# An attention and SwiGLU kernel: one ScalarE instruction without its wait for VectorE, three sums placed elsewhere in the last visits, one output scaled by another engine, and one step more in halves

## The chip, the cores and the metric

The kernel runs on one core of a Trainium2 chip. A core has five engines that work side by side, each through its own instructions in order: TensorE (PE; its weight loads are shown as PEld), VectorE (DVE), ScalarE (ACT), GpSimd (POOL) and SyncE (SP, which here only issues transfers). They wait for each other by semaphores. Matrix products are written to PSUM, which has eight banks of 512 fp32 values in each of 128 partitions; all else lies in SBUF. The metric is the device time of one execution in microseconds, the median of several runs.

## The reference

Attention without a mask over 8 batches and 12 heads, 448 positions of 64 values, then a SwiGLU feed-forward block over the 3584 tokens:

```python
def _attn_ref(q, k, v):                       # (8, 12, 448, 64) each
    scale = 1.0 / np.sqrt(q.shape[-1])
    scores = scale * np.matmul(q, k.transpose(0, 1, 3, 2))
    scores = scores - np.max(scores, axis=-1, keepdims=True)
    attn = np.exp(scores)
    attn = attn / (np.sum(attn, axis=-1, keepdims=True) + 1e-09)
    return np.matmul(attn, v).astype(np.float32)
...
def _moe_ref(x, w_gate, w_val, w_out):        # (3584, 768), (768, 1536) twice, (1536, 768)
    g = x @ w_gate
    silu = g * (1.0 / (1.0 + np.exp(-g)))
    val = x @ w_val
    return (silu * val @ w_out).astype(np.float32)
...
    x = np.ascontiguousarray(attn_out.transpose(0, 2, 1, 3)).reshape(B * S, H * D)
    return _moe_ref(x=x, **moe_kwargs)
```

## The kernel before

Heads are taken in 48 pairs, six pairs to a batch. Two batches make one block of 896 tokens for the feed-forward part; there are four such blocks. While TensorE works on the attention of later batches, it does the feed-forward of earlier ones in between, so that it always has something to do.

**Attention.** A pair's scores come in chunks (tile `s`, a PSUM tile of two banks from the pool `ps_s`, which has three buffers). ScalarE turns each chunk into exponentials (tile `E`, line 378, and line 403 for the first pairs). Then TensorE multiplies them with the values (tile `acc`, line 462; one bank of the pool `ps_f`, which has two buffers, for each head of the pair), VectorE forms the reciprocal of the row sums (line 504) and normalises (line 505, tile `xt`), and a transposing transfer from SyncE (lines 550 and 556) puts the result into `X`. Values are copied to their place by VectorE (`vo`, line 221).

**The plan.** A loop over `plan` visits three score chunks at a time and at most one pair's accumulation. From the visit called `base` on, what each visit does beside the attention is written out by hand in the list `VISITS`, 33 entries `(begins, nf, ng, no, ns)`: `nf` feed-forward steps, `ng` groups (`OutPair.wide`), `no` pieces of output (`plain_out`), `ns` sums taken from a queue (`add_sum`). The seven visits before `base` have their own list, `FIRST_STEPS`. All instructions are emitted in this order; nothing reorders them afterwards.

**A feed-forward step** (`Step`) forms 128 rows of the gate and value products for 384 or 512 tokens: six matmuls into `gp` (`X` times a gate weight), six into `vp`, both on line 610. ScalarE takes tanh of half of `gp` into `sg` (line 637 for a whole step), VectorE forms `t1 = (sg + 1) * gp` (line 687; the profile calls the tile `t`), then `hts = t1 * vp` (line 693). There are three forms. `run_fv` does one whole step, `run_pair` two interleaved, and `halves()` one step in two halves of the tokens: gate half 0 into one bank of a `ps_s` tile, gate half 1 into the other, then the value halves into two `ps_f` buffers. Its tanh is line 670, its t1 line 672, one of each for each half. A visit that has one step and an accumulation to do (`lone`) uses `halves()`; 17 steps do. `halves()` keeps a list `readers` of the instructions that have read the gate tile, and the helper `apart` takes away the dependencies of the next gate half's matmuls on them. The second tanh is not in that, so it waits for the first half's t1. `late_exp` holds exponentials back: in some visits of 384-token steps the third chunk's exponential is emitted only after the tanhs.

**Output.** `plain_out` multiplies `hts` with the output weights (tile `op`, line 729) and scales the result into `osb`, by VectorE (line 737) where the flag `by_vector` is set, otherwise by ScalarE (line 739). Other token chunks go in pairs through `OutPair.wide`, which forms four 128-row products with seven instead of eight half-size ones (tiles `og`, from `ps_s`, and `ob`, from `ps_f`, line 756). It needs sums of `hts` (four for each pair of chunks, lines 593 to 596) and of the output weights, and it has combines on VectorE (lines 813 and 822) between its products, for which later products wait.

**The last two blocks** are done after the visits by `Unit` (tile `un` from `ps_s`, `ub` from `ps_f`, line 912), in the same manner with seven products instead of eight. For that it needs sums of tokens, `token_sums` (lines 1095 to 1098, four sums of 1344 elements, in the queue `tsums6`), and sums of weights (lines 875 to 878, by GpSimd). The first combine of the first unit is line 961. The four token sums for the third block are popped from `tsums6` one by one in the last visits, at the end of each visit.

Of the kernel before, what the change touches and what calls it, by code (L numbers as in the profile page):

```python
# [12 lines left out]
AF = mybir.ActivationFunctionType  # L13
# [52 lines left out]
def kernel(  # L66
# [10 lines left out]
    nc = tc.nc  # L77
# [521 lines left out]
    class Step:  # L599
# [60 lines left out]
        def halves(self):  # L660
            w = self.at[2] // 2
            parts = [ds(i * w, w) for i in range(2)]
            gs = ps_s.tile([128, 2, 512], FP32, tag="s", name="gp")
            self.sg = fp.tile([128, 512], FP32, tag="sg", name="sg")
            self.t1 = fp.tile([128, 512], FP32, tag="t1", name="t1")
            readers = []
            for i, part in enumerate(parts):
                g = gs[:, i, 0:w]
                apart(self.group("g", gs[:, i], range(NCB), (i * w, w)), *readers)
                readers.append(nc.scalar.activation(self.sg[:, part], g, AF.Tanh, scale=0.5))  # L670
                readers.append(
                    nc.vector.scalar_tensor_tensor(self.t1[:, part], self.sg[:, part], 1.0, g, ALU.add, ALU.mult)
                )
            while late_exp:
                late_exp.pop(0)()
            vps = [ps_f.tile([128, 512], FP32, tag="f", name="vp") for _ in parts]
            for i, vp in enumerate(vps):
                self.group("v", vp, range(NCB), (i * w, w))
            for i, vp in enumerate(vps):
                self.close(i * w, w, vp)  # L680
# [38 lines left out]
    by_vector = [False]  # L719
# [281 lines left out]
    with tc.manual_schedule():  # L1001
# [41 lines left out]
        fvq = []  # L1043
# [8 lines left out]
        def add_block(i, visits):  # L1052
# [36 lines left out]
        ]  # L1089

        def token_sums(x, w, t, eng=nc.vector):
# [131 lines left out]
        g = FIRST * NC  # L1223
# [38 lines left out]
        for x, (chunks, todo) in enumerate(plan):  # L1262
            if not chunks and x > 1:
                break
            quads = [u for u in chunks if u[0] >= QUAD and u[1] == RU]
            split = 0 <= base - x < 3
            rests = [p0 for _, p0 in todo if p0 >= QUAD and not split]
            ordered = quads + [u for u in chunks if u not in quads]
            if (QUAD + 2, RU) in quads:
                ordered = ordered[1:] + quads  # L1270
            small = bool(quads)
            begins, nf, ng = VISITS[x - base][:3] if x >= base else (0, 0, 0)
            if begins > 2:
                add_block(begins, 0)
            lone = nf == 1 and bool(todo) and not split
            behind = []
            for n, (pr, c) in enumerate(ordered if x else []):
                if ng and not todo:
                    behind.append((pr, c, small))
                    continue  # L1280
                if n == 2 and ordered[n] in quads:
                    rests = open_products(rests, small)
                late = n == 2 and not todo and c < NC and pr < QUAD and bool(fvq) and not fvq[0].at[1]
                late = late or n == 2 and lone and not fvq[0].at[1]
                qk(pr, c, small, late)
            if (NPAIR - 1, KR - 1) in chunks:
                load_table("silu_and_others")
            open_products(rests, small)
            if x == 2:
                for t in qk16s:  # L1290
                    nc.vector.memset(t[96:128, 1], 0.0)
                turn_rests(0)
            end = min([y for y in adds if y > x] + [len(plan) + 1])
            if x == 0:
                add_block(0, end)
            early = [p0 for p0 in vcopies.get(x, []) if p0 < QUAD or x > base]
            for p0 in early if x <= base else []:
                copy_v(p0)
            entered = [pr for pr, c in chunks if c == 0]
            ready = []  # L1300
            for pr in entered:
                lead = [pr + 3] if pr + 3 < QUAD else [pr + 3, pr + 4] if pr + 3 == QUAD else [pr + 4]
                for p in lead:
                    if NPE <= p < NPAIR and p not in QPE:
                        ready.append(prep(p))
                if 14 <= pr + LA < NPAIR:
                    load_qk16(pr + LA, 1)
                if 12 <= pr + 3 < NPAIR:
                    load_v(pr + 3)
            for pr, c in chunks:  # L1310
                if c == 2 and (pr < NPE - 2 or pr + 2 in QPE):
                    prep(pr + 2)()
            if x in adds and 0 < x < base:
                add_block(adds[x], end - x)
            for _, p0 in todo:
                if split:
                    pv_split(p0)
                else:
                    pv(p0)
                if p0 < XPE:  # L1320
                    turns.append(p0)
                elif fvq and fvq[0].at[0] < p0 // NHP // NB - 1:
                    held.append(p0)
                else:
                    turn_x(p0)
            for turn in ready:
                if turn:
                    turn()
            for p0 in vcopies.get(x, []):
                if p0 not in early:  # L1330
                    copy_v(p0)
            for pr in entered:
                for w in wq.pop(pr, []):
                    emit(w)
            bare = not todo and bool(chunks) and x > 0
            if 0 < base - x <= len(FIRST_STEPS):
                n = FIRST_STEPS[x - base]
                gate_small[0] = bare
                if n > 1:
                    run_pair()  # L1340
                else:
                    run_fv(True)
            elif x < base:
                if bare and oq and not fvq:
                    carry -= run_o()
                elif bare:
                    gate_small[0] = True
                out_small[0] = not fvq and bool(oq) and any(p0 >= QUAD for _, p0 in todo)
                extra = 2 * fvq[0].time if bare and len(chunks) == 3 and fvq and not fvq[0].at[1] else 0
                carry = run_budget(left() / (end - x) + carry + extra) - extra  # L1350
            else:
                begins, nf, ng, no, ns = VISITS[x - base]
                gate_small[0] = bare
                out_small[0] = bool(no) and not bare
                for _ in range(ng):
                    run_group(behind)
                if lone:
                    fvq.pop(0).halves()
                    add_sum()
                elif bare_next(x):  # L1360
                    for _ in range(nf):
                        run_fv()
                else:
                    run_steps(nf)
                by_vector[0] = True
                for _ in range(no):
                    run_o()
                    out_small[0] = True
                out_small[0] = False
                if begins == 2:  # L1370
                    add_block(2, 0)
                ahead = {3: (x + 1, x + 2), 2: (), 1: ()}.get(len(VISITS) + base - x, (x + 1,))
                for p0 in [p for y in ahead for p in vcopies.get(y, [])]:
                    copy_v(p0)
                add_sum(ns)
                if x == len(VISITS) + base - 6:
                    wsum_space(rfree[:, 2 * NK * S :], 3)
                    for t in qk16s:
                        wsum_space(t[:].rearrange("p t c h d -> p (t c h d)"), 2)
                    wsum_space(Eall, 4)  # L1380
                    tsums6.extend(token_sums(X[KL - 1], S, t6))
            if len(VISITS) + base - x in (5, 3, 2, 1):
                tsums6.pop(0)()
            for u in {len(VISITS) + base - 6: range(2), len(VISITS) + base - 2: range(2, 3)}.get(x, []):
                weight_sums(u)
            while held and not fvq:
                turn_x(held.pop(0))
            while turns:
                turn_x(turns.pop(0))
# [138 lines left out]
```

## Time and profile before

| | |
|---|---|
| Time, median of 3 runs | 427.55 us (427.33 to 427.94) |
| The profiled execution: time | 428.34 us |
| The profiled execution: span of its instructions | 426.6 us |
| Busy in the span: TensorE, VectorE, ScalarE, GpSimd | 416.5, 268.7, 247.9, 224.8 us |
| First visit of `FIRST_STEPS` to the last step, some 84 to 243 us | 159 us, TensorE busy for 157.75 |
| Last visits, 243 to 277 us | 34 us, TensorE busy for 31.94 |
| The two unit blocks, 277 to 426 us | 149 us, TensorE busy for 145.24 |

Times in the profile are counted from the span's start. An engine is named with the line of the kernel and the tiles that an instruction writes and reads, and equal instructions that follow each other closely are merged into one row (x8). In square brackets stands how long the engine stood idle before the row, and what ended that. A matmul's end is modelled, so TensorE can look busy through a short wait; then the row is longer than another one of the same kind.

### The profile page before, as it was taken

Reading aid. Unit: us, or ns where it says so; the run is one execution under the profiler, and the core shown is the slowest. Engines: PE = TensorE matmul, PEld = TensorE weight load, DVE = VectorE, ACT = ScalarE, POOL = GpSimd, SP = SyncE. Lnnn points to the kernel's source line nnn. Section 1 sums busy time; section 2 is a strip of 40 time slices with the busy share of each in tenths; the row PEclk is TensorE's granted clock in tenths of the full one; section 3 lists DMA queues with packets and bytes.
Section 4 is the critical chain, followed back from the end, with each engine's and each line's share of the span. In section 5 each row is a group of like instructions: output and inputs, shape, how many; then the busy total and the mean of one; then the engine's idle time right before and its main releaser. Section 6 shows DMA issues by size and latency. Waiting matters only on the chain.

```text
span 426.6 us, 10831 instructions
## 1 busy us (share of the span) xinstructions
PE 416.5 (98%) x4328; PEld 258.8 (61%) x4328; DVE 268.7 (63%) x613; ACT 247.9 (58%) x384; POOL 224.8 (53%) x343
## 2 busy tenths in 40 slices
PE   8999999999999999999999999899999999999995
PEld 3666666555557776777767676455555655555564
DVE  4667662785777674567745587765765575565562
ACT  6975667646776574777647686545553225545221
POOL 8656625997899965599876625499800000000000
PEclk9999999999999999999999999999999999999999
DMA  9999999999999999999999836610000341000125
GB/s 138 180 201 200 200 176 184 140 162 184 174 189 159 157 208 170 118 167 159 125 166 171 98 76 95 155 35 0 2 1 20 93 116 33 0 2 0 38 79 145
DMA packets 108468, 50.30 MB, mean 118 GB/s; under 512 B 60416, under 2 KB 105344, under 8 KB 108416
## 3 DMA queue, kind: packets, MB, share of 16 engines
q0 software_dynamic: 46800, 24.56, 49.4%
q1 hardware_dynamic: 61344, 24.79, 31.9%
q8 instruction: 34, 0.56, 0.6%
q10 hardware_dynamic: 272, 0.25, 0.2%
q14 instruction: 18, 0.15, 0.1%
HBM read 49.55 MB, written 11.01 MB: 142 GB/s over the span
## 4 chain that ended last, share of the span: by engine, by line
PE 89%; DVE 4%; DMA 2%; POOL 2%; ACT 1%; issue 1%; ACTq 0%; DVEq 0%; POOLq 0%
PE gp L610 14%; PE un L912 13%; PE vp L610 11%; PE ub L912 10%; PE og L756 9%; PE acc L462 8%; PE ob L756 7%; PE s L356 5%; PE op L729 4%; PE acc L426 2%; PE op L1106 2%; PE s L393 2%; DMA qkraw<-in_k_dram 2%; PE s L368 1%; POOL qkraw L203 1%
## 5 line engine op out<-in xcount | busy, mean ns | idle before, releaser
L378 ACT ACTIVATE E<-s 128x896 f16<-128x896 f32 x126 | 106.7, 920 | 32.8 <-PE s L356 25.2
L610 PE MATMUL gp<-X,wg 128*128 128x256 f16 (+3 forms) x390 | 61.7, 304 | 0.0
L610 PE MATMUL vp<-X,wv 128*128 128x256 f16 (+3 forms) x390 | 58.6, 293 | 0.0
L240 POOL COPY qk<-qkraw 128x512 f16<-128x512 f16 x70 | 44.2, 678 | 24.9 <-DMA qkT<-qk 23.2
L180 POOL DMA_DIRECT2D vraw<-in_v_dram x72 | 44.1, 636 | 15.5 <-DMA wo<-in_moe_w_out_dram 8.2
L610 PEld LDWEIGHTS <-wv 128*128 128x128 f16 x432 | 40.6, 98 | 15.6
L180 POOL DMA_DIRECT2D qkraw<-in_k_dram x70 | 42.7, 627 | 7.1 <-DMA wo<-in_moe_w_out_dram 4.4
L403 ACT ACTIVATE E<-s 112x896 f16<-112x896 f32 x48 | 40.7, 917 | 8.1 <-PE s L393 8.1
L462 PEld LDWEIGHTS <-E 128*128 128x128 f16 (+2 forms) x1224 | 38.6, 98 | 10.4 <-issue 5.8
L462 PE MATMUL acc<-vo,E 128*128 128x65 f16 (+2 forms) x1224 | 43.3, 193 | 1.3 <-DVE hts L693 0.3
L610 PEld LDWEIGHTS <-wg 128*128 128x128 f16 x390 | 34.3, 98 | 16.4 <-issue 2.0
L756 PEld LDWEIGHTS <-hts 128*128 128x128 f16 x270 | 25.9, 98 | 16.0
L687 DVE SCALAR_TENSOR_TENSOR t<-sg,gp 128x384 f32<-128x384 f32 (+1 forms) x31 | 18.7, 617 | 22.8 <-ACT sg L637 22.8
L505 DVE TENSOR_TENSOR xt<-acc,R 128x256 f16<-128x256 f32 x72 | 30.5, 424 | 2.5
L203 POOL DMA_DIRECT2D qkraw<-in_q_dram x43 | 29.5, 686 | 4.5 <-DMA vraw<-in_v_dram 1.4
L693 DVE SCALAR_TENSOR_TENSOR hts<-t,vp 128x256 f16<-128x256 f32 (+3 forms) x65 | 29.1, 468 | 3.2 <-PE vp L610 1.2
L356 PE MATMUL s<-qkT 64*64 64x448 f16 (+1 forms) x288 | 30.5, 355 | 0.6 <-DVE osb L737 0.2
L977 ACT ACTIVATE silu<-un 128x448 f32<-128x448 f32 x24 | 13.0, 543 | 21.9 <-PE un L912 21.3
L961 DVE TENSOR_TENSOR un<-ub,kept 128x448 f32<-128x448 f32 x24 | 15.1, 630 | 16.6 <-ACT kept L958 10.3
L756 PE MATMUL og<-wo,hts 128*128 128x384 f16 x132 | 25.1, 326 | 0.0
L965 DVE TENSOR_TENSOR kept<-ub,kept 128x448 f32<-128x448 f32 x24 | 15.0, 624 | 15.0 <-PE ub L912 15.0
L221 DVE COPY vo<-vraw 128x512 f16<-128x512 f16 (+1 forms) x48 | 20.3, 425 | 4.2 <-DMA vraw<-in_v_dram 4.1
(210 smaller groups left out, 735.6 us busy)
## 6 DMA issues: line engine op xcount, KB each, us to landing
vraw<-in_v_dram POOLq DMA_DIRECT2D x72, 64.0 KB, 4.9
qkraw<-in_q_dram POOLq DMA_DIRECT2D x39, 112.0 KB, 4.5
qkraw<-in_k_dram POOLq DMA_DIRECT2D x68, 64.0 KB, 5.0
wg<-in_moe_w_gate_dram POOLq DMA_DIRECT2D x8, 288.0 KB, 9.9
wv<-in_moe_w_val_dram POOLq DMA_DIRECT2D x8, 288.0 KB, 10.3
wo<-in_moe_w_out_dram POOLq DMA_DIRECT2D x2, 1152.0 KB, 18.9
out_dram<-osb SPq DMA_DIRECT2D x7, 288.0 KB, 4.7
out_dram<-osb SPq DMA_DIRECT2D x9, 192.0 KB, 2.9
```

What stands on the lines that cost most here:

```text
L180: eng.dma_start(dst[ts(s, 64)], rows)
L203: nc.gpsimd.dma_start(dst, flat.rearrange("h (p c) d -> p h (c d)", c=NC))
L240: nc.gpsimd.tensor_copy(dst.rearrange("p c h d -> p h c d"), src)
L356: nc.tensor.matmul(s[ts(half, m), hx, 0:S].rearrange("p (c q) -> p c q", q=P), lhsT=t[ts(hx, 64), ds((c + low(pr, hx)) * 128 + half * m, m ...
L378: nc.scalar.activation(e, s[:, :, 0:S], AF.Exp, scale=sm_scale)
L403: nc.scalar.activation(e[:, :, 0:S], s[0:P, :, 0:S], AF.Exp, scale=sm_scale)
L462: nc.tensor.matmul(acc[ds(lo, m), ts((j + pr % 2) % (KR + 1), D + 1)], lhsT=e[rows, ds(hx * S + j * 128 + lo, m)], rhs=Vts[pr % NV][rows, ...
L505: nc.vector.tensor_tensor(xt[:, :, hx], a4[:, :, 0:D], r[:].unsqueeze(2).to_broadcast([128, KR + 1, D]), ALU.mult,)
L610: nc.tensor.matmul(dst[:, 0:w], lhsT=wslice(kind, self.fb, cb), rhs=X[kk][:, cb, ds(c0 + lo, w)], start=(cb == 0), stop=(cb == NCB - 1),)
L693: nc.vector.scalar_tensor_tensor(self.hts[:, self.fb, ds(lo, w)], self.t1[:, ds(lo, w)], 0.5 * HS, vp[:, 0:w], ALU.mult, ALU.mult)
L756: nc.tensor.matmul(dst, lhsT=lhs(n), rhs=rhs(n), start=first and n == 0, stop=n == NH - 1, skip_group_check=True)
L912: mm = nc.tensor.matmul(dst, lhsT=lhs[:, n], rhs=rhs[:, n], start=first and n == 0, stop=n == NK - 1, skip_group_check=True,)
```

## The change

Five edits:

1. In `halves()` the second tanh no longer depends on the first half's t1. `readers[1:2]` is that instruction when the second half is emitted, and empty for the first half.
2. The last of `FIRST_STEPS`, the visit before `base`, runs its single step by `halves()` and no longer by `run_fv`.
3. In `VISITS` the fourth entry from the end has one sum more and the third from the end one less: one of the `hts` sums is emitted one visit earlier.
4. `by_vector` is not set for the visit with index 26, so its piece of output is scaled by ScalarE.
5. Of the four pops of `tsums6`, those of the visits with 5, 3, 2 and 1 left become those with 5, 2, 1 and 1 left: the second is emitted one visit later, and the third together with the fourth in the last visit.

```diff
@@ -667,7 +667,10 @@
             for i, part in enumerate(parts):
                 g = gs[:, i, 0:w]
                 apart(self.group("g", gs[:, i], range(NCB), (i * w, w)), *readers)
-                readers.append(nc.scalar.activation(self.sg[:, part], g, AF.Tanh, scale=0.5))
+                tanh = nc.scalar.activation(self.sg[:, part], g, AF.Tanh, scale=0.5)
+                for reader in readers[1:2]:
+                    tc.declare_no_dep(tanh.ins, reader.ins, reason="another bank")
+                readers.append(tanh)
                 readers.append(
                     nc.vector.scalar_tensor_tensor(self.t1[:, part], self.sg[:, part], 1.0, g, ALU.add, ALU.mult)
                 )
@@ -1084,8 +1087,8 @@
             (0, 2, 0, 0, 0), (0, 1, 0, 0, 0), (0, 1, 0, 0, 0), (0, 1, 0, 0, 0), (3, 1, 0, 0, 0),
             (0, 1, 0, 0, 0), (0, 1, 0, 0, 0), (0, 2, 0, 0, 0), (0, 1, 0, 0, 0), (0, 1, 0, 0, 0),
             (0, 0, 1, 0, 0), (0, 1, 0, 0, 0), (0, 1, 0, 0, 0), (0, 1, 0, 0, 0), (0, 2, 0, 0, 0),
-            (4, 0, 0, 1, 1), (0, 0, 0, 1, 1), (0, 0, 0, 1, 2), (0, 0, 1, 0, 0), (0, 0, 0, 1, 1),
-            (0, 0, 0, 0, 1), (0, 0, 1, 0, 0), (0, 0, 0, 0, 0),
+            (4, 0, 0, 1, 1), (0, 0, 0, 1, 1), (0, 0, 0, 1, 2), (0, 0, 1, 0, 0), (0, 0, 0, 1, 2),
+            (0, 0, 0, 0, 0), (0, 0, 1, 0, 0), (0, 0, 0, 0, 0),
         ]
@@ -1338,8 +1341,10 @@
                 gate_small[0] = bare
                 if n > 1:
                     run_pair()
+                elif x < base - 1:
+                    run_fv(True)
                 else:
-                    run_fv(True)
+                    fvq.pop(0).halves()
             elif x < base:
@@ -1362,7 +1367,7 @@
                         run_fv()
                 else:
                     run_steps(nf)
-                by_vector[0] = True
+                by_vector[0] = x != len(VISITS) + base - 7
                 for _ in range(no):
                     run_o()
                     out_small[0] = True
@@ -1379,7 +1384,7 @@
                         wsum_space(t[:].rearrange("p t c h d -> p (t c h d)"), 2)
                     wsum_space(Eall, 4)
                     tsums6.extend(token_sums(X[KL - 1], S, t6))
-            if len(VISITS) + base - x in (5, 3, 2, 1):
+            for _ in range({5: 1, 2: 1, 1: 2}.get(len(VISITS) + base - x, 0)):
                 tsums6.pop(0)()
```

## The prediction

> **What bounds the kernel now.** I read the page first (busy shares, chain of waits), then the list of who waited for whom, then the timeline of the visits that the change touches.
>
> ```profile
> PE 416.5 (98%) x4328; PEld 258.8 (61%) x4328; DVE 268.7 (63%) x613; ACT 247.9 (58%) x384; POOL 224.8 (53%) x343
> ...
> PEclk9999999999999999999999999999999999999999
> ...
> PE 89%; DVE 4%; DMA 2%; POOL 2%; ACT 1%; issue 1%; ACTq 0%; DVEq 0%; POOLq 0%
> ```
>
> TensorE is busy 98% of the span at full granted clock and holds 89% of the chain: the other engines matter only where TensorE waits for them. Busy time hides short waits, since the ends of matmuls are modelled. So I looked in the timeline for TensorE rows that last longer than equal rows without a wait.
>
> ```profile
> ACT sg L670 <- DVE t L672: 8.2, 16, 0.5
> ```
>
> L670 is the tanh of a step in halves. The second tanh of such a step sat idle for 0.5 us, 16 times, until VectorE had done t1 (L672) of the first half. The timeline shows what this costs; start and duration are the first two columns:
>
> ```profile
> 119.76 0.55 PE L356 MATMUL s<-qkT 64*64 64x448 f16 x8
> ...
> 130.35 1.15 PE L610 MATMUL gp<-X,wg 128*128 128x192 f16 x12
> 131.11 0.33 ACT L670 ACTIVATE sg<-gp 128x192 f32<-128x192 f32 x1 [0.19 <-PE gp L610]
> 131.47 0.35 DVE L672 SCALAR_TENSOR_TENSOR t<-sg,gp 128x192 f32<-128x192 f32 x1
> 131.92 0.33 ACT L670 ACTIVATE sg<-gp 128x192 f32<-128x192 f32 x1 [0.48 <-DVE t L672]
> 132.15 3.34 ACT L378 ACTIVATE E<-s 128x896 f16<-128x896 f32 x4
> 132.69 0.80 PE L356 MATMUL s<-qkT 64*64 64x448 f16 x8
> ```
>
> The exponential held back behind the tanhs starts at 132.15. It frees the score buffer that the last of these eight score matmuls needs: they take 0.80 instead of the 0.55 of the same eight at 119.76. Where no exponential is held back, VectorE's last read is late instead, and the next heads' accumulation waits for it (1.39 against 1.25):
>
> ```profile
> 166.93 1.25 PE L462 MATMUL acc<-vo,E 64*128 64x65 f16 x32
> ...
> 190.33 0.38 ACT L670 ACTIVATE sg<-gp 128x256 f32<-128x256 f32 x1 [0.55 <-DVE t L672]
> 191.61 1.39 PE L462 MATMUL acc<-vo,E 64*128 64x65 f16 x32
> ```
>
> The last visits have one long wait:
>
> ```profile
> 249.44 0.37 PE L356 MATMUL s<-qkT 64*128 64x448 f16 x2 [0.20 <-DVE osb L737]
> ...
> 267.32 1.26 DVE L596 TENSOR_TENSOR hsum<-hts,hsum 128x768 f16<-128x768 f16 x1
> 268.51 1.56 DVE L1096 TENSOR_TENSOR vraw<-X,vraw 128x1344 f16<-128x1344 f16 x1
> 269.34 0.38 PE L356 MATMUL s<-qkT 64*64 64x448 f16 x4
> 269.99 0.54 DVE L822 SCALAR_TENSOR_TENSOR p<-og,p 128x384 f32<-128x384 f32 x1
> 270.64 0.56 DVE L813 SCALAR_TENSOR_TENSOR og<-p,ob 128x384 f32<-128x384 f32 x1
> 271.26 1.14 PE L756 MATMUL ob<-E,hsum 128*128 128x384 f16 x6 [1.54 <-DVE og L813]
> ...
> 276.88 1.22 DVE L1098 TENSOR_TENSOR qkraw<-X,vraw 128x1344 f16<-128x1344 f16 x1
> 279.73 0.63 DVE L961 TENSOR_TENSOR un<-ub,kept 128x448 f32<-128x448 f32 x1 [0.53 <-PE ub L912]
> ```
>
> Two sums (L596, L1096) stand in VectorE's queue before the combines L822 and L813, for which TensorE idles.
>
> **The change, part by part.**
>
> *Second tanh freed.* In the changed program it waits for TensorE alone, in all 18 steps. It can start when its half of gp is done: at 131.50 instead of 131.92 (gp's last matmul is issued at 131.26, its result comes some 0.2 later). In the 256-wide steps the gain is about 0.5 (tanhs back to back). Held exponential, second t1 and both closing products move with it. What TensorE lost in these steps, row by row against the undisturbed row: the x8 scores at 132.69, 141.27, 153.73, 170.30, 178.87, 186.71: 0.80 or 0.79 against 0.55, six times, 1.46; the x6 scores at 157.39 and 182.54: 1.04 against 0.74, 0.60; the x32 accumulations at 158.26, 191.61, 196.13, 228.59, 233.25: 1.34, 1.39, 1.33, 1.45, 1.44 against 1.25, 0.70; x40 at 210.99: 1.48 against 1.16, 0.32. Sum 3.08. Each loss is smaller than the 0.34 to 0.52 by which the tanh moves, so I count them as gone, except the 0.19 at 233.25: there the trace puts the second tanh's idle 0.82 down to TensorE's vp, not to t1. **2.9 us**; both ends 0 (first rival) and 3.3 (with 0.23 of late starts at 210.99 and 233.25). Behind the earlier tanhs nothing else is short: operands of coming heads land 14 us or more before their first scores here, values over 5 us before their copies, so transfers don't take the place of the wait. The first tanh now names a VectorE wait, but for a read two steps older.
>
> *One more step in halves* (the last before the first of VISITS, 116.86 to 119.45 now). Six gp and six vp matmuls of 512 columns become twelve each of 256: 1.31 per group instead of 1.29 in the chain, **-0.03** with its 12 more weight loads inside. Two tanhs of 0.38 for one of 0.60, t1 and hts 0.42 each half for 0.69: VectorE would close both halves by some 120.1, before 120.47 now, and the accumulation it releases starts at 120.24. There is no wait in this visit to win; the 0.35 at 124.77 is in the following step, which stays whole. Bounds -0.1 and 0.
>
> *One output scaled by ScalarE* (the second of four). VectorE ended it at 249.39, behind two normalisations. ScalarE's exponentials run out at 248.83, the product is done at 248.78, 0.33 more (192-wide tanh) makes 249.17. The scores at 249.44 could start at 249.06 without any wait (six take 0.74, here 1.12), so 0.24 of 0.38 is won. The exponential behind it on ScalarE starts at 249.18 instead of 249.15. **0.24**; bounds 0 and 0.38.
>
> *Sums moved.* L596 goes to VectorE's idle 0.58 before 264.57 (beside a still GpSimd the same sum took 0.56 at 252.86). L822 can then start when the copies of values end at 267.41, L813 at 268.45 when ob is done, ending 269.01; TensorE goes on at 269.63 (scores plus 0.29, as at 266.99 to 267.28). 1.63 won there; L1096 now follows the last combine, 0.85 in an idle stretch. But L1097 moves too, behind the next normalisation: L1097 and L1098 then stand in a row before L961, whose slack was 0.53. On TensorE's new times: normalisation ends 276.96 - 1.63 = 275.33, two sums of S each, the last normalisation 1.18, L961 0.63, 0.09 of handing over: the ub matmuls that need L961 start at 277.23 + 2S, before it was 280.79. Kept of the 1.63: 3.56 - 2S, at most 1.63. S is 0.85 beside a still GpSimd (L1097 now) and 1.22 or 1.56 beside its adds, which run here; I take 1.39: **0.78**, bounds 0.44 and 1.63. The Trainium skill (SBUF — State Buffer, section Who interferes with whom) says that a VectorE instruction with two SBUF inputs and a GpSimd instruction that reads SBUF exclude each other, and that whichever began first holds the shared ports for its whole length. By that S could be an add of 0.91 plus 0.85, 1.76, and only 0.04 would be kept; no sum in the trace was that long.
>
> Sum: 2.9 - 0.03 + 0.24 + 0.78 = 3.9. The profiled execution took 428.34 us with a span of 426.6, 0.8 above the median of the runs; from the units on TensorE stands still for 0.15 at 296.83 and hardly again, so all of it reaches the end. 428.34 - 3.9 = 424.4 for such an execution, 427.55 - 3.9 = **423.7** for the median.
>
> **Rivals.**
> - *The second tanh is released no earlier.* At 232.03 it began as TensorE's vp half ended, not gp. If that were the rule, the tanh at 190.33 would start at 190.46 and the 2.9 would vanish: 427.55 - 1.0 = 426.6. Against: the other sixteen of the seventeen began 0.09 us after t1's end, most of them (131.92, 190.33) while vp's half was still running. Chance 0.10.
> - *Reads that overlap slow each other.* Tanh and t1 would read two banks of one tile at once; 0.1 to 0.2 us more on each would eat the thin margins (0.30 of 0.37 at 157.39, 0.44 of 0.52 at 210.99), about half: 425.1. Against: at 135.33 and 135.90 both engines read such a pair, at the usual 0.46 and 0.51. Chance 0.10.
> - *The last visits give nothing*, S near 1.76: 427.55 - 3.15 = 424.4. Chance 0.06.
> - *Slower:* the two sums in a row wait for a whole unit of four GpSimd adds (3.65 us from 281.56), not one: S = 4.5, which keeps 3.56 - 9.0 = -5.4 in place of 0.78; 427.55 + 5.4 - 3.1 = 429.9. It decides from S = 3.3. Against: L1098 took 1.22 beside such a run. Chance 0.04.
>
> That the wait is not removed at all is no case: the changed program no longer has it.
>
> **How the numbers follow.** The forecast has 0.70, its own range 422.3 (all upper bounds) to 424.6. The range is 422.2 to 426.4: it takes in overlapping reads and idle last visits, and leaves out the tanh case, the slower one and a tail. Within 0.2% (0.86 us, about what a measurement here can tell from no change) lies half of the tanh case, 0.05; slower 0.04; faster 0.91.
>
> **What would show it.** Right: no wait of L670 for L672; the x8 scores back at 0.55, x32 at 1.25 or less; no TensorE idle before the ob of the last pair, but a new one of about 0.85 before the ub matmuls that follow the first L961. Wrong: a second tanh that starts with the end of vp's half; tanhs or t1 longer by 0.1; scores still waiting for the held exponential; L1097 and L1098 over 1.6 each.

## The result, and the profile after

The changed kernel took 422.56 us (median of 6 runs, 421.66 to 424.61), the kernel before 427.79 beside it (6 runs, 427.33 to 430.02): a ratio of 0.987, 95% interval 0.9836 to 0.9905. Forecast were 423.7, range 422.2 to 426.4. A second measurement gave 421.95 (4 runs), which is below that range, against 428.38 (11 runs): 0.9852, interval 0.9829 to 0.9874. The profiled execution took 421.66 with a span of 419.9; the one before had 428.34 and 426.6.

In the changed kernel every line from the tanh on is three lower down: tanh L670 (unchanged), first product t1 L675, closing products L696, output by VectorE L740 and by ScalarE L742, out products L759, combines L816 and L825, weight sums L878 to L881, `ub` matmuls L915, first combine of the units L964, token sums L1098 to L1101.

The page of the changed kernel, busy times and chain of waits:

```profile
PE 413.5 (98%) x4340; PEld 259.5 (62%) x4340; DVE 270.0 (64%) x614; ACT 247.8 (59%) x386; POOL 224.4 (53%) x343
...
PEclk9999999999999999999999999999999999999999
...
PE 94%; DVE 2%; ACT 1%; DMA 1%; issue 1%; SPq 0%; DVEq 0%
```

TensorE has 94% of the chain in place of 89%, VectorE 2% in place of 4%. The view of line L670 (engine, operation, count, durations in ns; then who ended its engine's idle time):

```profile
L670 ACT ACTIVATE sg<-gp x36: 330/383/418, 117.2 to 231.4; 128x256 f32<-128x256 f32 x20, 128x192 f32<-128x192 f32 x16
...
  PE gp L610: 2.4, 12
```

No tanh waits for VectorE or for `vp` any more. Durations are those of before (330/383/432), and so are t1's (353/414/423 in L675, 353/420/422 in L672), although the two engines now read the two banks at once: the overlapping reads cost nothing that these durations show.

The timeline of the first step in halves behind which an exponential is held back (start, duration, engine, line):

```profile
130.22 0.33 ACT L670 ACTIVATE sg<-gp 128x192 f32<-128x192 f32 x1
130.58 0.85 DVE L675 SCALAR_TENSOR_TENSOR t<-sg,gp 128x192 f32<-128x192 f32 x2
130.71 0.33 ACT L670 ACTIVATE sg<-gp 128x192 f32<-128x192 f32 x1 [0.17 <-PE gp L610]
130.94 0.91 ACT L378 ACTIVATE E<-s 128x896 f16<-128x896 f32 x1
131.81 0.55 PE L356 MATMUL s<-qkT 64*64 64x448 f16 x8
132.06 2.54 ACT L378 ACTIVATE E<-s 128x896 f16<-128x896 f32 x3 [0.20 <-PE s L368]
...
136.31 0.86 PE L356 MATMUL s<-qkT 64*128 64x448 f16 x6
136.41 0.35 DVE L696 SCALAR_TENSOR_TENSOR hts<-t,gp 128x192 f16<-128x192 f32 x1
136.67 0.35 DVE L696 SCALAR_TENSOR_TENSOR hts<-t,vp 128x192 f16<-128x192 f32 x1
```

The second tanh follows the first by 0.49 (it was 0.81), and the eight score matmuls are back at 0.55. New is the row at 136.31: six scores of the visit behind it take 0.86 instead of 0.74. ScalarE now stands idle for 0.20 at 132.06, because it is ahead of the scores, and so its three exponentials end later relative to TensorE than the unbroken four of before. The tanhs of the whole steps behind them and VectorE's products are late too: the last two of the six scores start 0.05 after the closing product of 136.41 has ended, and the accumulation behind them 0.05 after that of 136.67. Together that is 0.18.

In a step of 512 tokens both tanhs form one row, and the accumulation behind it has none of its old excess:

```profile
186.74 0.68 ACT L670 ACTIVATE sg<-gp 128x256 f32<-128x256 f32 x2
...
188.75 1.12 PE L462 MATMUL acc<-vo,E 64*128 64x65 f16 x32
```

The last visits:

```profile
264.72 1.15 PE L759 MATMUL ob<-E,hsum 128*128 128x384 f16 x6
...
269.96 0.91 POOL L881 TENSOR_TENSOR E<-wv,E 128x384 f16<-128x384 f16 x1
270.37 1.22 DVE L1100 TENSOR_TENSOR qkraw<-X 128x1344 f16<-128x1344 f16 x1
270.84 1.52 POOL L878 TENSOR_TENSOR E<-wg 128x384 f16<-128x384 f16 x1
271.51 1.56 DVE L1101 TENSOR_TENSOR qkraw<-X,vraw 128x1344 f16<-128x1344 f16 x1
272.43 1.41 POOL L879 TENSOR_TENSOR E<-E,wg 128x384 f16<-128x384 f16 x1
274.09 0.62 DVE L964 TENSOR_TENSOR un<-ub,kept 128x448 f32<-128x448 f32 x1
274.76 0.73 PE L915 MATMUL ub<-qkraw 128*128 128x448 f16 x3 [0.33 <-DVE un L964]
```

The idle of 1.54 ahead of the last pair's `ob` (264.72) is gone. Two token sums now stand in a row ahead of the combine at 274.09, and the `ub` matmuls wait for it.

To see where the time went I put equal TensorE matmuls of the two traces side by side and noted how much earlier the changed kernel starts each:

```
TensorE rows, by their start before                    start before - start after
130.35 first step in halves behind an exponential       0.83
191.61 (steps of 384 tokens behind it)                  2.9
237.25 (last step in halves behind it)                  4.66
251.70                                                  4.94
271.26 ob of the last pair                              6.53
280.79 ub behind the first combine, and on              6.02
end of the span                                         6.7
```

So the steps in halves gave 3.83, the visit with the output by ScalarE 0.27, the last pair's wait 1.6, and 0.50 was given back. The first 0.83 were there before any changed instruction runs but the one more step in halves (0.76 at 18.21 already, in the start-up), and 0.66 lies behind the last matmul. These two differ from execution to execution, as the experiments show, and do not belong to the change.

### The profile page after: what moved, and what is told of

It reads as the page before. It is cut to its first block, busy times and chain, and to the rows that moved or that the text cites. A ratio compares the mean times of both kernels' runs of the same rounds, so it can differ in the third digit from the quotient of the medians.

```text
span 419.9 us, 10841 instructions
## 1 busy us (share of the span) xinstructions
PE 413.5 (98%) x4340; PEld 259.5 (62%) x4340; DVE 270.0 (64%) x614; ACT 247.8 (59%) x386; POOL 224.4 (53%) x343
## 4 chain that ended last, share of the span: by engine, by line
PE 94%; DVE 2%; ACT 1%; DMA 1%; issue 1%; SPq 0%; DVEq 0%
PE gp L610 14%; PE un L915 12%; PE vp L610 12%; PE og L759 10%; PE ub L915 10%; PE acc L462 8%; PE ob L759 8%; PE s L356 5%; PE op L732 4%; PE s L393 2%; PE acc L426 2%; PE op L1109 2%; PE s L368 1%; PE tp L324 1%; ACT E L403 1%; DMA rk<-in_k_dram 1%
## 5 line engine op out<-in xcount | busy, mean ns | idle before, releaser
L240 POOL COPY qk<-qkraw 128x512 f16<-128x512 f16 x70 | 43.0, 661 | 18.7 <-DMA qkT<-qk 18.2
L462 PE MATMUL acc<-vo,E 128*128 128x65 f16 (+2 forms) x1224 | 42.1, 193 | 0.6 <-DVE osb L816 0.3
L759 PEld LDWEIGHTS <-hts 128*128 128x128 f16 x270 | 25.9, 98 | 16.0
L696 DVE SCALAR_TENSOR_TENSOR hts<-t,vp 128x256 f16<-128x256 f32 (+3 forms) x66 | 30.7, 465 | 3.4 <-PE vp L610 1.2
L356 PE MATMUL s<-qkT 64*64 64x448 f16 (+1 forms) x288 | 28.8, 352 | 0.0
L964 DVE TENSOR_TENSOR un<-ub,kept 128x448 f32<-128x448 f32 x24 | 15.1, 630 | 16.1 <-ACT kept L961 10.3
L759 PE MATMUL og<-wo,hts 128*128 128x384 f16 x132 | 25.0, 326 | 0.0
```

The lines of the kernel that those rows point to most:

```text
L240: nc.gpsimd.tensor_copy(dst.rearrange("p c h d -> p h c d"), src)
L356: nc.tensor.matmul(s[ts(half, m), hx, 0:S].rearrange("p (c q) -> p c q", q=P), lhsT=t[ts(hx, 64), ds((c + low(pr, hx)) * 128 + half * m, m ...
L462: nc.tensor.matmul(acc[ds(lo, m), ts((j + pr % 2) % (KR + 1), D + 1)], lhsT=e[rows, ds(hx * S + j * 128 + lo, m)], rhs=Vts[pr % NV][rows, ...
L696: nc.vector.scalar_tensor_tensor(self.hts[:, self.fb, ds(lo, w)], self.t1[:, ds(lo, w)], 0.5 * HS, vp[:, 0:w], ALU.mult, ALU.mult)
L759: nc.tensor.matmul(dst, lhsT=lhs(n), rhs=rhs(n), start=first and n == 0, stop=n == NH - 1, skip_group_check=True)
```

## The experiments

Each edit alone comes first, put into the kernel before. Shifts of TensorE, which say how much earlier an equal matmul starts, are read against the trace of before as in the table. They resolve 0.03 us, where medians of a few runs scatter by 0.5; but each comes from one execution.

**e1: the freed tanh alone.**

```diff
+                tanh = nc.scalar.activation(self.sg[:, part], g, AF.Tanh, scale=0.5)
+                for reader in readers[1:2]:
+                    tc.declare_no_dep(tanh.ins, reader.ins, reason="another bank")
+                readers.append(tanh)
```

> The kernel before with the first edit alone (no second tanh waits for VectorE's read of the first half). Theory: 3.9 us faster, since TensorE gained 3.86 between 128.99 and 237.25 in the two traces, nearly all of it in the steps in halves; from 427.8 that is 423.9. The prediction's own term was 2.9, which would make 424.9. Rival: the gain stands only together with the moved sums, because the wait before the last pair's outputs would swallow it: then the span falls by less than 2. What the trace should show by the theory: no idle of L670's tanh on L672, the x8 scores at 0.55, the x32 accumulations at 1.12 to 1.25, the last pair's wait of 1.54 still there at its full length, and no wait before the ub matmuls behind the first combine.

Measured: 424.12 (6 runs) against 427.75 (29 runs), ratio 0.9908 (0.9888 to 0.9927). TensorE gains 3.52 between 130.35 and 237.25, and later only 0.24 at 249.63, which e3 explains; the wait of 1.54 is untouched. The gain does not need the moved sums.

**e5: the freed tanh in the steps of 512 tokens alone.**

```diff
-                for reader in readers[1:2]:
+                for reader in readers[1:2] if self.at[2] == 512 else []:
```

> The kernel before with the second tanh freed in the steps of 512 tokens alone (halves of 256); the steps of 384 tokens (halves of 192), behind which an exponential is held back, keep their wait. Theory: the accumulations of 32 and 40 matmuls behind the 512 steps go from 1.33-1.48 to 1.12-1.25, 1.6 us faster in all (426.2 from 427.8), and the x8 and x6 scores behind the 384 steps stay at 0.80 and 1.04; so 2.3 of the 3.9 belongs to the held exponential. By the prediction's rows (0.70 + 0.32, against 2.06) it would be 1.0 faster. Rival: what counts is the sum of the shifts, and TensorE meets the waits of the 384 steps later or earlier, so that neither part alone is worth what its rows show: under 0.5 or over 2.5.

Measured: 425.83 (10 runs) against 427.69 (13), 0.9961 (0.9944 to 0.9978). TensorE gains 1.8 in these steps; the others keep their loss, as a step of 384 tokens of this kernel shows:

```profile
177.06 0.33 ACT L670 ACTIVATE sg<-gp 128x192 f32<-128x192 f32 x1 [0.48 <-DVE t L675]
...
177.84 0.79 PE L356 MATMUL s<-qkT 64*64 64x448 f16 x8
```

So 1.8 of the 3.5 belongs to the accumulations of the 512 steps and 1.7 to the held exponentials of the 384 steps. The rows that the prediction added up give 0.74 and 2.15. In the 512 steps the rows of before, held against the true undisturbed 1.12 (x32) and 1.14 (x40), lose 0.27, 0.21, 0.34, 0.33 and 0.32, and three accumulations start late by 0.15, 0.09 and 0.09: 1.80. In the 384 steps the x8 and x6 scores gain 1.48 and 0.58 as forecast, and twice 0.18 is given back in the visit behind, at 136.31 and 172.86: 1.70.

**e2: the moved sums alone.**

```diff
-            if len(VISITS) + base - x in (5, 3, 2, 1):
+            for _ in range({5: 1, 2: 1, 1: 2}.get(len(VISITS) + base - x, 0)):
```

(with the two entries of `VISITS` that move the sum of L596)

> The kernel before with the moved sums of the last visits alone. Theory: TensorE gains 1.5 to 1.6 before the outputs of the last pair and gives some 0.5 back before the ub matmuls behind the first combine, 1.1 us faster in all: 426.7 from 427.8. The prediction's term was 0.78 (427.0). Rival (an exclusive port, S = 1.76): 0.04 kept, no change. The two token sums that stand in a row should take 1.2 to 1.6 us each; the first half of the program should stay as it was.

Measured: 426.62 (12 runs) against 427.75, 0.9968 (0.9955 to 0.9981). The trace: 1.61 gained at the `ob`, 0.49 lost at the `ub`, 1.12 kept; the medians say 1.13. VectorE's rows there:

```profile
275.36 1.22 DVE L1097 TENSOR_TENSOR qkraw<-X 128x1344 f16<-128x1344 f16 x1
276.50 1.56 DVE L1098 TENSOR_TENSOR qkraw<-X,vraw 128x1344 f16<-128x1344 f16 x1
277.98 0.17 DVE L504 RECIPROCAL R<-acc 128x4 f32<-128x4 f32 x1
...
279.08 0.62 DVE L961 TENSOR_TENSOR un<-ub,kept 128x448 f32<-128x448 f32 x1
```

The sums are 1.22 and 1.56, together the 2 x 1.39 of the forecast. But each row starts 0.08 before the one ahead of it has ended (275.36 + 1.22 = 276.58, and the next starts at 276.50). Adding durations end to end counts four such overlaps twice, 0.32.

**e3: the output by ScalarE alone.**

```diff
-                by_vector[0] = True
+                by_vector[0] = x != len(VISITS) + base - 7
```

> The kernel before with one output product scaled by ScalarE in place of VectorE. Theory: the wait of the scores at 249.44 on that product goes, 0.25 us faster (0.24 was the prediction's term, 0.28 is what the traces show there): 427.5 from 427.8. Rival: ScalarE's exponential behind it becomes late and takes it back: no change, with a new wait of TensorE on the exponential in the next two visits.

Measured: 428.19 (10 runs) against 427.75, 1.0001 (0.9986 to 1.0016): nothing. The shift at 249.63 is 0.27, which looks like the expected gain, but e1, e2, e4 and e5, which keep VectorE there, have 0.24. So most of the wait was an event of the one execution of before that was profiled. The timeline of before, at that place:

```profile
246.66 0.96 POOL L875 TENSOR_TENSOR qk<-wv 128x384 f16<-128x384 f16 x1
246.77 1.26 DVE L593 TENSOR_TENSOR qkraw<-hts 128x768 f16<-128x768 f16 x1
...
249.05 0.34 DVE L737 TENSOR_SCALAR osb<-op 128x192 f32<-128x192 f32 x1
```

and of e2, which has the same instructions there:

```profile
245.70 0.90 POOL L875 TENSOR_TENSOR qk<-wv 128x384 f16<-128x384 f16 x1
246.74 0.55 DVE L593 TENSOR_TENSOR qkraw<-hts 128x768 f16<-128x768 f16 x1
...
248.99 0.88 PE L356 MATMUL s<-qkT 64*128 64x448 f16 x6
249.09 0.36 DVE L737 TENSOR_SCALAR osb<-op 128x192 f32<-128x192 f32 x1 [0.16 <-PE op L729]
```

GpSimd's adds of the weights happened to run a microsecond later in the first, so that one stood in the way of VectorE's sum (1.26 instead of 0.55), and the two normalisations and the output behind it were late. Without that the six scores wait 0.13 with VectorE and 0.10 with ScalarE: the edit is worth 0.03.

**e4: the one more step in halves alone** (its second tanh still waits).

```diff
-                else:
+                elif x < base - 1:
                     run_fv(True)
+                else:
+                    fvq.pop(0).halves()
```

> The kernel before with one more step in halves (the one before the first visit with a normalisation), whose second tanh still waits for VectorE. Theory: nothing to win at its place, no wait of TensorE in that step before or after; 0 to 0.1 us slower by the twelve more matmuls of half the width: 427.8 to 427.9. Rival: the step was moved to halves because VectorE's last read comes earlier and takes away the 0.35 to 0.40 us that the accumulation at 124.77 waits: then 0.3 faster, and that wait is shorter.

Measured: 427.60 (10 runs) against 427.75, 0.9988 (0.9972 to 1.0003). At its own place nothing changes by more than 0.16 in either direction, and the wait in the step behind stays. But at 159.43, 40 us later, TensorE gains 0.20, and the last pair's wait is 1.02 instead of 1.54. The second is chance: the copies of values ended some 0.5 sooner, and GpSimd's adds lay elsewhere; before, e1, e3 and e5 all have 1.54. Where an execution goes as that of e4, the moved sums of e2 would win about 0.5 less, by estimate. The first recurs, see e10.

**e6: the last token sum behind the first combine** (in the changed kernel, as the next ones).

```diff
-            for _ in range({5: 1, 2: 1, 1: 2}.get(len(VISITS) + base - x, 0)):
+            for _ in range({5: 1, 2: 1, 1: 1}.get(len(VISITS) + base - x, 0)):
...
+        items["T3"] = (DVE_, 0.85, ["D1_0"], tsums6.pop(0))
+        eng, us, behind, fn = items["P4_0"]
+        items["P4_0"] = (eng, us, behind + ["T3"], fn)
```

> The changed kernel, with the last of the four token sums (L1101) moved from ahead of VectorE's first combine behind it, in front of the next thing that needs it. Theory: the combine starts some 1.5 us sooner, the new wait of 0.50 before the ub matmuls goes, 0.4 to 0.5 us faster than the changed kernel: 422.1 from 422.56. Rival: the sum then delays GpSimd's next unit or the second combine, and the wait comes back there: no change, with a new TensorE wait behind 276.

Measured: 421.82 (4 runs), 0.9864 (0.9846 to 0.9881) of before. Against the changed kernel's trace the wait ahead of the `ub` is gone, 0.50, another 0.16 is won at 290.81, and 0.27 is given back at 298.75 in the same kind of wait: 0.39 in all. The medians (421.82 here, 422.56 and 421.95 for the changed kernel, from other measurements) cannot tell that from nothing.

**e7: the one more step in halves a visit later**, where TensorE waits for `hts` (0.21 by the first profile row below).

```diff
-                elif x < base - 1:
-                    run_fv(True)
                 else:
-                    fvq.pop(0).halves()
+                    run_fv(True)
...
+                elif x == base:
+                    fvq.pop(0).halves()
+                    add_sum(2)
```

> The changed kernel, with the one more step in halves moved on by one visit: the step at the first visit with a normalisation runs in halves, the one before it whole. Theory: TensorE waits 0.32 us at 124.25 for the hts of that step, and a step in halves ends VectorE's work earlier, so the wait goes: 0.3 us faster than the changed kernel, 422.3. Rival: its two tanhs come behind the same exponentials and VectorE is behind the normalisation, so the wait stays: no change.

Measured: 422.00 (4 runs), 0.9868 (0.985 to 0.9886). The changed kernel has at that visit

```profile
124.25 1.11 PE L462 MATMUL acc<-vo,E 64*128 64x65 f16 x31 [0.21 <-DVE hts L696]
```

and this one, with no wait,

```profile
123.98 0.98 DVE L696 SCALAR_TENSOR_TENSOR hts<-t,vp 128x256 f16<-128x256 f32 x2
...
125.01 1.12 PE L462 MATMUL acc<-vo,E 64*128 64x65 f16 x32
```

TensorE's shift there against the changed kernel is 0.39. The edit also places two sums of the output weights (`add_sum(2)`) behind the step. They were not what TensorE waited for: in the changed kernel the one ahead of the step's first product ended at 122.60, and that product waited for its tanh until 122.69. So the step was split one visit too early to win anything at its own place.

**e8 and e12: the last sum later, and the step at `base` in halves too.** The edits of the two runs are the same. They split the step of e7 but do not make the one before it whole again, as the expectations have it: 19 steps run in halves (38 tanhs in L670, where the changed kernel and e7 have 36).

> The changed kernel with both of the last two edits (last token sum behind the first combine, and the step in halves moved on by one visit). Theory: their gains lie in different stages and add: 0.7 to 0.8 us faster than the changed kernel, 421.8. Rival: the end takes one of them back: 422.2.

> The changed kernel with the last token sum behind the first combine and the step in halves moved on by one visit, once more, beside the changed kernel on one chip. Theory: 0.5 (no wait before the ub matmuls) + 0.39 (no wait for hts two visits after the first one) = 0.9 us faster than the changed kernel. Rival: the earlier measurement, 421.85 against 422.56, holds: 0.7 or less, some of it given back later.

Measured (e8): 421.85 (4 runs), 0.9865 (0.9847 to 0.9882); e12: 421.37 (5 runs), 0.9847 (0.9823 to 0.9871), beside 421.95 for the changed kernel. In the trace of e12 both gains stand, 0.39 and 0.50 (+0.16 at 290.81, -0.25 at 298.75), 0.80 in all. In that of e8 0.22 of the first is lost again 2 us later, ahead of the `vp` matmuls that the changed kernel starts at 126.57; e10, below, has such a wait at another place. The intervals of the two kernels overlap: the version is better by its traces and by its medians, though not surely so.

**e9: the changed kernel again, and e10: without the step in halves and the output by ScalarE.**

> The changed kernel once more, beside its variants on one chip, to compare them by their own medians. Sum of the parts as the traces of the single edits showed them: 3.5 (tanh) + 1.1 (sums) + 0.03 (output by ScalarE) + 0 (one more step in halves) = 4.65 below the kernel before, 423.1 from 427.75. If the first measurement (422.56, 5.2 below) is repeated, some 0.5 more comes from the edits together than from each alone.

> The changed kernel without its step in halves and without the output by ScalarE: only the freed tanh and the moved sums. Theory: these two carry all of it, within 0.1 us of the changed kernel on the same chip. By the prediction's terms it would be 0.2 slower. Rival: the one more step in halves wins something only beside the freed tanh (the sum of the parts is 0.5 short of the whole): then 0.3 to 0.5 slower.

Measured: 421.95 (4 runs) and 422.73 (6 runs), 0.9852 and 0.9874 (0.9852 to 0.9896). The trace of e9 repeats that of the first measurement from the first steps in halves on: 3.82, 0.27, 1.61 and -0.49. The trace of e10 loses 0.11 at 157.49, 0.21 at 205.51 in a wait of `vp` that appears at changing places, and 0.03 at 244.70. The first is the place of e4. In e10:

```profile
156.36 0.35 DVE L696 SCALAR_TENSOR_TENSOR hts<-t,vp 128x192 f16<-128x192 f32 x1
...
156.90 0.35 DVE L696 SCALAR_TENSOR_TENSOR hts<-t,vp 128x192 f16<-128x192 f32 x1 [0.19 <-DVE hts L696]
```

and in the changed kernel:

```profile
155.70 0.71 DVE L696 SCALAR_TENSOR_TENSOR hts<-t,vp 128x192 f16<-128x192 f32 x2
```

The second of these closing products starts 0.19 to 0.21 after the first has ended in all six kernels without the added step (before, e1, e2, e3, e5, e10) and follows at once in all eight with it. Its waits are the same in both programs. What differs is how many instructions VectorE has behind it by then. So the step in halves is worth 0.1 to 0.2 us by something that it does 40 us later; what holds the product up stays open.

The medians show more than the traces. e10 is 0.78 slower than e9 in the same measurement, and each of its six runs is slower than all four of e9. Of the 1.04 between their two profiled spans, 0.34 lies behind the start-up and ahead of the last matmul. Whether the rest of the 0.78 belongs to the two edits is open. Against before, e9 is 6.4 faster, more than the 4.65 that its expectation adds up; the traces explain 5.0 (see below).

**e11: GpSimd's adds held back behind the sums.** One more add of 16 columns reads the last token sum, so that GpSimd cannot start its next unit before it; the columns are overwritten by that unit.

```diff
+        nc.gpsimd.tensor_add(wsum_at[12][:, 0:1, 0:16], t6[3][:, 0:1, 0:16], t6[3][:, 0:1, 0:16])
         for u in range(3, NFB):
             items[f"W_{u}"] = (POOL_, 3.65, [f"W_{u - 1}"], lambda u=u: weight_sums(u))
```

> The changed kernel, with GpSimd's next unit of four adds (those that run at 270.84, 272.43, 273.80, 274.67) held back until the fourth token sum is written, by one small add of 16 columns that reads this sum. Theory (a VectorE instruction with two SBUF inputs and a GpSimd add take turns, each for its whole length): with no add to take turns with, the sum at 271.51 takes 0.85 in place of 1.56, the one before it 0.85 to 1.22, the combine behind them starts 0.7 to 1.0 sooner and the wait of 0.50 before the ub matmuls goes; the adds, now alone, take 0.91 in place of 1.52 and 1.41. Rival (each sum is slower for another reason, its operands or its place behind the normalisation): the sums stay at 1.2 and 1.56 and the wait stays. The time may lose again what GpSimd's unit is late for: up to 0.5 faster if nothing waits for it, slower if a later unit does.

Measured: 422.08 (4 runs, 420.89 to 423.78), 0.9858 (0.9829 to 0.9888). Its timeline:

```profile
273.06 0.85 DVE L1100 TENSOR_TENSOR qkraw<-X 128x1344 f16<-128x1344 f16 x1
273.83 0.85 DVE L1101 TENSOR_TENSOR qkraw<-X,vraw 128x1344 f16<-128x1344 f16 x1
...
275.05 0.91 POOL L878 TENSOR_TENSOR E<-wv 128x384 f16<-128x384 f16 x1
...
276.97 0.73 PE L915 MATMUL ub<-qkraw 128*128 128x448 f16 x3
```

Both sums take 0.85, the adds 0.91, and the `ub` matmuls do not wait: a gain of 0.50 there. (This execution lay 1.5 behind in the start-up and 1.0 more at 87 us, long before the edit.) With the adds out of the way both sums take what such a sum takes alone, and the adds, away from the sums, too: each had made the other slow. The medians (422.08 here, 421.95 for e9) do not show the gain of 0.50.

## Why the prediction was right, and which sizes were off

- **What bounds the kernel** was read rightly: TensorE, and only the waits that end last there.
- **Second tanh freed, 2.9.** The mechanism held as told. The size was 3.5 alone (e1), from two errors of opposite sign. The row taken as undisturbed (x32 at 166.93, 1.25) is itself disturbed: it waits for an output of L813 and is still 1.25 in the changed kernel. Rows of 1.12 stood in the same trace, at 138.02 and 206.58. That, the late starts kept for the upper bound, and the accumulation at 233.25 that was left out make 1.80 of 0.74 in the 512 steps. In the 384 steps the sentence that behind the earlier tanhs nothing else is short was wrong: ScalarE runs ahead, stands idle for 0.20, and twice 0.18 comes back as a new wait; the 0.09 counted at 158.26 is not won by e1, but comes with the step in halves. That makes 1.70 of 2.15.
- **The rival that `vp` releases the second tanh** fell: no tanh waits for `vp` any more. The idle of 0.82 at 232.03 was no accident, since e2 and e3 have it too (0.83 there in e2); it went with the wait on VectorE. Why it was longer than t1 is not settled.
- **Overlapping reads** fell: durations as before.
- **One more step in halves, -0.03.** Right for its own visit, wrong in sum: 0.1 to 0.2 won at 158, where a pause of VectorE that no wait explains is gone (e4, e10).
- **Output by ScalarE, 0.24.** This step failed. It was worked out from a wait that belonged to one execution; 0.03 is what is left (e3 against the traces that keep VectorE).
- **Sums moved, 0.78.** The time S of a sum was right to the hundredth (2.78 for two), but by luck: 1.39 is the mean of 1.22 and 1.56, and the two sums happened to take one of each. The 1.63 was right (1.61), and the rest was mis-sized by the end-to-end addition: 1.12 was kept. The Trainium skill (SBUF — State Buffer, section Who interferes with whom) says that a VectorE instruction with two SBUF inputs and a GpSimd instruction that reads SBUF exclude each other for a whole instruction. The trace agrees: in the four rows from 270.37 on, 1.22 is 0.85 and 0.37 of the 0.50 that the add from 269.96 still had to run, 1.56 is 0.85 and 0.71 of an add of 0.91, and the adds grew to 1.52 and 1.41 in turn; in e11, with no add beside them, all are 0.85 and 0.91. What failed in the prediction was the price put on that rule: 1.76 for both would be two sums that each wait for a whole add from its first instant; one sum met the second half of an add, and the other waited 0.71. So the rival that the last visits give nothing was the right mechanism with the wrong phase.
- **The slower rival**, a sum that waits for four adds, fell: one at a time.
- **The sum.** 3.9 forecast. The traces give 3.83 (tanh and step in halves) + 0.03 + 1.12 = 5.0, and the medians of the first measurement 5.2. Alone the parts are 3.5, 0.2, 0.03 and 1.12, 4.85 in all, so in the traces the edits hardly change each other's worth. The second measurement gives 6.4 (5.4 to 7.3 by its interval), more than the traces explain; what the rest is stays open. All terms but the output by ScalarE were forecast too small, and the first measurement lies 0.36 inside the fast end of the range. The forecast's own range, 422.3 to 424.6, does not follow from its bounds: all upper ones make 422.2, and 2.9 with the lower bounds of the other three makes 424.3.

## What to carry to other kernels

Before a row counts as undisturbed, look for the shortest of its kind in the whole trace, and before a wait is priced, ask whether a free-running engine (here GpSimd, whose adds start when a transfer or a buffer lets them) could have put it there in this one execution. Work moved between two engines that share something costs by the phase in which they meet, so price it between the work alone and the work plus one whole instruction of the other (here the most was 0.71 of an add of 0.91). Where a wait is taken from one engine's queue, follow the next rows of that engine until it idles: that is where part of the gain comes back.

## What the runs showed of the hardware

- VectorE's sums of two SBUF operands and GpSimd's adds take turns, and both rows get longer: 1.22 and 1.56 for 0.85, 1.52 and 1.41 for 0.91. An addition of 0.71 appears at other sizes too (1.26 for 0.55 at 246.77 before).
- Rows of VectorE overlap: one that waits for nothing starts some 0.08 us before the end that the profile shows for the one ahead (276.50 against 276.58 in e2).
- Equal stretches of program differ: the first scores behind the start-up began between 17.41 and 19.05 us in 14 traces, and from the start of the last matmul to the end of the span it takes 3.86 to 4.57 us, with the same instructions there.
- In six traces out of six without the added step in halves, one VectorE product near 157 us starts 0.19 to 0.21 us after everything that the profile shows it to wait for; in eight out of eight with such a step it does not. The reason is not known.
